# Seven block products beside each FFN1 step, and block sums a few steps earlier

## The chip, the cores and the metric

One core of one Trainium2 chip. The metric is the device time of one launch in microseconds. TensorE (PE) does matrix products into PSUM; VectorE (DVE), ScalarE (ACT) and GpSimd (POOL) do the rest, and SyncE (SP) issues output transfers. Each engine works through its own list of instructions in order, and semaphores keep the lists in step.

## The reference

Attention over 8 batches, 8 heads, 576 queries of 64 elements, with 16 beacon keys that all queries see and 576 causal ones. Its output is laid out as 4608 tokens of 512, and a feed-forward layer follows:

```python
x = attn_out.transpose(0, 2, 1, 3).reshape(B * S, H * D)      # 4608 x 512
h = x @ w_in                                                  # 4608 x 2048
g = np.where(h > 0.0, h, np.exp(np.minimum(h, 0.0)) - 1.0)
return g @ w_out                                              # 4608 x 512
```

## The kernel before, in words

Tokens are cut into ten tiles: two of 256, then eight of 512 (t = 2 to 9). The order of every engine's work is written out by hand. Short words name the operations, with their arguments behind dots, and a function `run` emits them one by one; what is emitted first stands first on its engine. For tiles 0 to 2 the words are one long string. From there on a loop goes over blocks b = 3 to 10. Block b does FFN1 of tile b, FFN2 of tile b − 1, and parts of the attention of batches b and b + 1; blocks 8 and 9 have no attention left, and block 10 has only FFN2 of tile 9.

A block has 16 steps, i = 0 to 15, one for each 128 columns of h:

- `F` (line 436): four matmuls of 128 x 512 into one of two PSUM banks, `hps`.
- `e` (446, ScalarE): the exponential of the bank. `r` (451, VectorE): min(e, 1) − 1. `g` (459, VectorE): the larger of h and r, into the tile `gt`. Then the bank is free for the F two steps later.
- `S`, `x`, `m` (277, 287, 303): scores, their exponential on ScalarE, the causal mask on VectorE. `T`, `ck` (235, 256): transposes of q and k and their copy on ScalarE. `L`, `W`, `R` (314): row sums and products with v, R being those of the last 64 queries of a batch. `n` (347, 350): reciprocal of the row sums as exp(−ln) on ScalarE. `M` (384, 404, VectorE): the scaled output, which is x of FFN1. Twelve steps carry such work: eight with scores (0, 1, 4, 5, 7, 8, 11, 12) and four with transposes and products (2, 6, 9, 13).

FFN2 of a tile is a product of 2 x 2 blocks (tokens halved, 2048 halved by alternating chunks, 512 halved) in Winograd's form, with seven block products where eight would be plain. Each product is a phase `ph` = 0 to 6 of 16 matmuls: two halves `qd` of 128 tokens, eight chunks `c` each. Phases 0, 2, 4, 6 write one PSUM bank and phases 1, 3, 5 another, some of them adding to what is there. `Q` (531) emits the matmuls, and `J` what follows a phase: a copy to `sm` on ScalarE (540; phases 0, 2, 3), a sum with it on VectorE (547; phases 1, 4, 5) or a copy on ScalarE (545; phase 6), the last two kinds with a store of 256 KB on SP's queue.

The left operands are blocks of g and sums of them. `Z` (489, VectorE) makes four sums, each in two halves of four chunks: sum 3 into `s3`, sums 1, 2 and 4 in place. Sum 2 overwrites the operand of phase 0 and is the operand of phase 2; sum 4 does the same between phases 1 and 5; sum 1 is for phase 3, sum 3 for phase 4. `wt` (also 489) makes the sums of the weights, once.

Before the change `Q` has a phase and a half as arguments and emits eight matmuls. A list `HS` gives the 14 steps that have one; steps 6 and 13 have none. `J` follows the second half of its phase in the same step, and `Z` stands behind `J`, in the steps that `SUMS` gives. Phases 0 to 6 so end in steps 1, 3, 5, 8, 10, 12 and 15. Words in a step are emitted as F, e, r, g, then Q and J, then Z, then the attention work.

Of the kernel before, what the change touches and what calls it, by code (L numbers as in the profile page):

```python
# [17 lines left out]
def kernel(  # L18
# [21 lines left out]
    R = 6  # L40
# [29 lines left out]
    NFC = DF // P  # L70
# [31 lines left out]
    NPR = NFC // 2  # L102
# [381 lines left out]
    def A(t, h_, j, i):  # L484
        v_ = gh[t, h_].rearrange("p (c j) (i w) -> p c j i w", j=2, i=2)
        return v_[:, :, j, i, :]
# [19 lines left out]
    def Z(t, n, h_):  # L506
# [8 lines left out]
        else:  # L515
# [3 lines left out]
    PH = [(0, (0, 0), B11, True), (1, (1, 0), B21, True), (0, (0, 0), T2, False), (1, (0, 1), T1, True),  # L519
          (0, None, B12, False), (1, (1, 0), B22, False), (0, (1, 1), T4, False)]  # L520

    @step
    def Q(t, ph, qd):

        if (t, 0) not in xy:
            for n_ in (0, 1) if t % 2 == 0 else (1, 0):
                xy[t, n_] = psum.tile([P, 2, HM], FP32, tag="ops", name="ops")
        n_, src, wt_, first = PH[ph]
        for c in range(NPR):
            lw = s3[:, c] if src is None else A(t, c // HP, *src)[:, c % HP]  # L530
            nc.tensor.matmul(  # L531
                out=xy[t, n_][:, qd, :], lhsT=lw[:, P * qd:P * (qd + 1)], rhs=wt_[:, c, :],
                start=(first and qd == 0 and c == 0), stop=(c == NPR - 1), skip_group_check=True)
# [33 lines left out]
    def run(names):  # L567
        for word in names.split():
            f, *args = word.split(".")
            op[f](*[a if a in "ABR" else int(a) for a in args])  # L570
# [30 lines left out]
    M.2.0.1 e.2.7 M.2.0.0 F.2.9 wt.1.1 S.3.0.0 e.2.9 S.2.3.2 lv.3 G.1.0.2 r.2.7 g.2.7 x.3.0.0 x.2.3.2  # L601
    F.2.11 wt.2.0 S.3.0.1 e.2.11 x.3.0.1 r.2.9 m.3.0.0 g.2.9 m.2.3.2 r.2.11 g.2.11 s.1.1 S.2.3.3 m.3.0.1
    F.2.10 wt.2.1 x.2.3.3 G.1.0.3 e.2.10 S.3.0.2 m.2.3.3 o.1.0 x.3.0.2 S.3.0.3 F.2.12 wt.4.0 r.2.10 m.3.0.2 g.2.10
    L.2.1 e.2.12 W.2.1.0 x.3.0.3 s.1.0 r.2.12 F.2.14 wt.4.1 g.2.12 m.3.0.3 n.2.1 M.2.1.0 F.2.13 e.2.14
    T.3.1 W.2.1.1 e.2.13 r.2.14 R.2 ck.3.1 T.3.2 g.2.14 r.2.13 F.2.15 g.2.13 M.2.1.1 n.2.R M.2.R
    e.2.15 r.2.15 ck.3.2 g.2.15
    """)

    def T_(b, p):
        if b < B:  # L610
            run(f"cb.{b}.{p} T.{b}.{p} ck.{b}.{p}")

    def SC(b, p, g0):
        if b < B:
            for g_ in (g0, g0 + 1):
                run(f"S.{b}.{p}.{g_} x.{b}.{p}.{g_} m.{b}.{p}.{g_}")

    def LW(b, g):
        run(f"L.{b}.{g} W.{b}.{g}.0 n.{b}.{g} M.{b}.{g}.0")

    def WR(b, g):
        run(f"W.{b}.{g}.1" + g * f" R.{b}" + f" M.{b}.{g}.1" + g * f" n.{b}.R M.{b}.R")

    SLOTS = [0, 1, 2, 4, 5, 6, 7, 8, 9, 11, 12, 13]
    HS = [0, 1, 2, 3, 4, 5, 7, 8, 9, 10, 11, 12, 14, 15]
    SUMS = {0: [(-1, 1, 1)], 2: [(-1, 2, 0)], 3: [(-1, 2, 1)], 5: [(-1, 4, 0)], 7: [(-1, 4, 1)],
            11: [(0, 3, 0)], 13: [(0, 1, 0)], 15: [(0, 3, 1)]}
    for b in range(3, NT // TT + 2):
        todo = {}
        if b < B:  # L630
            todo = dict(zip(SLOTS, [
                lambda: SC(b, 1, 0), lambda: SC(b, 1, 2), lambda: (T_(b, 3), LW(b, 0)),
                lambda: SC(b, 2, 0), lambda: SC(b, 2, 2), lambda: (T_(b + 1, 0), WR(b, 0)),
                lambda: SC(b, 3, 0), lambda: SC(b, 3, 2), lambda: (T_(b + 1, 1), LW(b, 1)),
                lambda: SC(b + 1, 0, 0), lambda: SC(b + 1, 0, 2), lambda: (T_(b + 1, 2), WR(b, 1))]))
        if b == 3:
            run("wt.3.0 wt.3.1 Z.2.3.0 Z.2.1.0 Z.2.3.1")
        for i in range(NFC):
            if b < len(tiles):
                run(f"F.{b}.{i} e.{b}.{i} r.{b}.{i} g.{b}.{i}")  # L640
            if i in HS:
                n_ = HS.index(i)
                run(f"Q.{b - 1}.{n_ // 2}.{n_ % 2}")
                if n_ % 2:
                    run(f"J.{b - 1}.{n_ // 2}")
            for dt_, n_, h_ in SUMS.get(i, []):
                if b + dt_ < len(tiles):
                    run(f"Z.{b + dt_}.{n_}.{h_}")
            if i in todo:
                todo[i]()  # L650
            if i == 3 and b + 1 < B:
                run(f"lk.{b + 1} lv.{b + 1}")
# [28 lines left out]
```

## Time and profile before

| what | value |
|---|---|
| time, median of 3 | 377.95 us (377.32 to 377.96) |
| profiled execution | 377.59 us, its span 375.9 us |
| PE busy | 352.2 us |
| DVE busy | 286.5 us |
| ACT busy | 253.7 us |
| block with attention (b=5, first F to first F) | 184.01 to 224.37 us |
| block without attention (b=9) | 330.38 to 358.09 us |

In rows of the profile, L531 is line 531 of the kernel, `ops<-wt,gt` reads tiles wt and gt and writes ops, and a bracket gives the idle time before and what ended it. Rows in order of time begin with the start and the duration, both in us. Matmuls are pipelined: the duration of a row reaches beyond the start of the next, so the distance of starts is what one costs. Rows of stretches give the stretch, its length, and busy time of each engine with its number of instructions in brackets. Waits give the sum in us, how many, and the longest.

### The profile page before, as it was taken

Reading aid. Unit: us, or ns where it says so; the run is one execution under the profiler, and the core shown is the slowest. Engines: PE = TensorE matmul, PEld = TensorE weight load, DVE = VectorE, ACT = ScalarE, POOL = GpSimd, SP = SyncE. Lnnn points to the kernel's source line nnn. Section 1 sums busy time; section 2 is a strip of 40 time slices with the busy share of each in tenths; the row PEclk is TensorE's granted clock in tenths of the full one; section 3 lists DMA queues with packets and bytes.
Section 4 is the critical chain, followed back from the end, with each engine's and each line's share of the span. In section 5 each row is a group of like instructions: output and inputs, shape, how many; then the busy total and the mean of one; then the engine's idle time right before and its main releaser. Section 6 shows DMA issues by size and latency. Waiting matters only on the chain.

```text
span 375.9 us, 11164 instructions
## 1 busy us (share of the span) xinstructions
PE 352.2 (94%) x4811; PEld 219.8 (58%) x4811; DVE 286.5 (76%) x675; ACT 253.7 (67%) x383; POOL 68.5 (18%) x100
## 2 busy tenths in 40 slices
PE   7989999999888999899989999899989998998985
PEld 3567666454555665566655666566645665665674
DVE  2448877779788697787877787868878888888861
ACT  2999996887676867697668768686767354344321
POOL 8876630410330004100510040000000000000000
PEclk9999999999999999999999999999999999999998
DMA  8999999963298019900973057001000100110112
GB/s 117 170 186 197 179 190 196 74 103 81 17 59 149 3 58 95 151 6 30 102 101 77 14 71 70 28 2 59 31 28 2 60 28 30 47 39 29 56 58 85
DMA packets 65201, 28.89 MB, mean 77 GB/s; under 512 B 41088, under 2 KB 63616, under 8 KB 65152
## 3 DMA queue, kind: packets, MB, share of 16 engines
q0 software_dynamic: 54720, 18.49, 44.7%
q1 hardware_dynamic: 9856, 9.57, 7.7%
q8 instruction: 37, 0.61, 0.7%
q10 hardware_dynamic: 576, 0.13, 0.2%
q14 instruction: 12, 0.10, 0.1%
HBM read 37.22 MB, written 9.44 MB: 124 GB/s over the span
## 4 chain that ended last, share of the span: by engine, by line
PE 57%; DVE 20%; ACT 10%; issue 5%; POOL 3%; DMA 3%; ACTq 0%; DVEq 0%; POOLq 0%
PE hps L436 22%; PE ops L531 18%; DVE gt L459 5%; PE lt L314 5%; PE sc L277 5%; ACT et L287 4%; DVE r L451 4%; PE ops L468 3%; DVE xT L384 3%; PE tp L235 3%; DVE osb L547 3%; DVE gt L489 2%; DMA kst<-in_k_dram 2%; PE ut L314 2%; ACT rl L350 2%
## 5 line engine op out<-in xcount | busy, mean ns | idle before, releaser
L436 PE MATMUL hps<-xT,w_in 128*128 128x512 f16 (+1 forms) x640 | 147.7, 359 | 4.4 <-DVE gt L459 3.5
L446 ACT ACTIVATE e<-hps 128x512 f32<-128x512 f32 x144 | 86.5, 601 | 53.4 <-PE hps L436 52.2
L287 ACT ACTIVATE et<-sc 128x832 f16<-128x832 f32 x128 | 104.2, 873 | 21.3 <-PE sc L277 21.3
L459 DVE TENSOR_TENSOR gt<-hps,r 128x512 f16<-128x512 f32 x144 | 99.6, 691 | 6.5 <-PE sc L277 0.5
L531 PEld LDWEIGHTS <-gt 128*128 128x128 f16 x768 | 74.5, 98 | 38.0 <-DVE gt L489 11.5
L436 PEld LDWEIGHTS <-w_in 128*128 128x128 f16 x640 | 56.3, 97 | 51.7 <-issue 12.0
L451 DVE TENSOR_SCALAR r<-e 128x512 f16<-128x512 f32 x144 | 62.5, 434 | 16.2 <-ACT e L446 14.4
L531 PE MATMUL ops<-wt,gt 128*128 128x256 f16 x384 | 50.5, 273 | 9.3 <-DVE gt L489 9.3
L303 DVE TENSOR_TENSOR et<-et,triu 128x256 f16<-128x256 f16 (+2 forms) x164 | 39.8, 271 | 23.3 <-ACT et L287 21.8
L531 PE MATMUL ops<-w_out,gt 128*128 128x256 f16 x384 | 49.1, 273 | 0.0
L277 PE MATMUL sc<-qk 64*128 64x208 bf16 (+9 forms) x528 | 36.6, 249 | 2.0 <-ACT et L287 1.1
L256 ACT COPY qk<-tp 128x1152 bf16<-128x1152 bf16 x29 | 32.5, 1134 | 3.9 <-PE tp L235 3.8
L132 POOL DMA_DIRECT2D v<-in_v_dram x40 | 34.2, 885 | 4.6 <-DMA kst<-in_k_dram 2.6
L489 DVE TENSOR_TENSOR gt<-gt 128x1024 f16<-128x1024 f16 x48 | 32.5, 682 | 0.1
L277 PEld LDWEIGHTS <-qk 64*128 64x128 bf16 x528 | 19.0, 94 | 22.6 <-issue 16.0
L314 PEld LDWEIGHTS <-v 128*32 128x32 f16 x1248 | 21.2, 94 | 9.2 <-issue 2.5
L127 POOL DMA_DIRECT2D v<-in_beacon_v_dram x8 | 4.3, 534 | 115.0 <-PE ut L314 115.0
L384 DVE TENSOR_TENSOR xT<-lt,rl 128x448 f16<-128x448 f32 (+6 forms) x28 | 10.6, 419 | 15.4 <-ACT rl L350 15.4
L547 DVE TENSOR_TENSOR osb<-ops,sm 128x512 f32<-128x512 f32 x24 | 16.4, 682 | 5.6 <-issue 4.6
L540 ACT COPY sm<-ops 128x512 f32<-128x512 f32 x24 | 14.1, 586 | 8.3 <-PE ops L531 8.3
L314 PE MATMUL ut<-et,v 128*32 128x64 f16 (+6 forms) x840 | 16.9, 224 | 1.1 <-issue 0.6
L468 PE MATMUL ops<-w_out,gt 128*128 128x512 f16 x64 | 16.5, 380 | 0.0
(55 smaller groups left out, 249.2 us busy)
## 6 DMA issues: line engine op xcount, KB each, us to landing
out_dram<-osb SPq DMA_DIRECT2D x36, 256.0 KB, 2.2
qst<-in_q_dram POOLq DMA_DIRECT2D x6, 576.0 KB, 6.5
kst<-in_k_dram POOLq DMA_DIRECT2D x6, 576.0 KB, 9.4
v<-in_v_dram POOLq DMA_DIRECT2D x24, 128.0 KB, 5.1
w_in<-in_moe_w_in_dram POOLq DMA_DIRECT2D x16, 128.0 KB, 5.3
w_out<-in_moe_w_out_dram POOLq DMA_DIRECT2D x4, 512.0 KB, 11.0
v<-in_v_dram POOLq DMA_DIRECT2D x8, 112.0 KB, 3.3
v<-in_v_dram POOLq DMA_DIRECT2D x8, 80.0 KB, 5.2
```

What stands on the lines that cost most here:

```text
L132: nc.gpsimd.dma_start(out=st[b][2][r0:r0 + n, j, :, :], in_=v[b, :, ilo[j]:ilo[j] + n, :].rearrange("h s d -> s h d"),)
L256: nc.scalar.copy(out=t[:, :, NB:SK].rearrange("c i (p r) -> c i p r", r=R), in_=tps[b, p][:, :, 0:S].rearrange("c i (r p) -> c i p r", r=R))
L277: nc.tensor.matmul(out=s[:, h, a - c0:e - c0], lhsT=t[D * h:D * (h + 1), 1, P * j:P * (j + 1)], rhs=t[D * h:D * (h + 1), 0, NB + qa + a - ...
L287: nc.scalar.activation(out=ets[b, p][:, :, GW * g:GW * (g + 1)], in_=sc[b, p, g][:, :, 0:GW], func=AFT.Exp, bias=0.0, scale=SCALE)
L303: nc.vector.tensor_tensor(out=o, in0=o, in1=triu[0:kc[j], :, t0:t0 + e - a], op=ALU.mult)
L314: nc.tensor.matmul(out=t[32 * i:32 * (i + 1), a - qa:e - qa], lhsT=ones[0:kc[j], :] if half is None else v16[0:kc[j], j, h, 32 * half:32 * ...
L436: nc.tensor.matmul(out=h[:, n_, :], lhsT=w_in16[:, cc, P * fc:P * (fc + 1)], rhs=xt[k][:, cc, a - TT * k:e - TT * k], start=(cc == 0), sto ...
L446: nc.scalar.activation(out=eb[t, i], in_=flat(hp[t, i]), func=AFT.Exp, bias=0.0, scale=1.0)
L451: nc.vector.tensor_scalar(out=rb[t, i], in0=eb[t, i], scalar1=1.0, scalar2=1.0, op0=ALU.min, op1=ALU.subtract)
L459: nc.vector.tensor_tensor(out=gh[k][:, i % UN, :], in0=flat(hp[t, i]), in1=rb[t, i], op=ALU.max)
L489: nc.vector.tensor_tensor(out=o_, in0=a_, in1=b_, op=op_)
L531: nc.tensor.matmul(out=xy[t, n_][:, qd, :], lhsT=lw[:, P * qd:P * (qd + 1)], rhs=wt_[:, c, :], start=(first and qd == 0 and c == 0), stop= ...
```

## The change

`Q` has a first and a last matmul, counted through all seven phases (112), and each of the 16 steps emits seven. `J` is emitted in the step in which the last matmul of its phase was emitted, behind that step's matmuls: phases 0 to 6 in steps 2, 4, 6, 9, 11, 13 and 15. The second half of sum 4 moves from step 7 to 6, and the first half of sum 1 from 13 to 12. For tile 2 the three sums that stood at the start of block 3 move into the written order: `Z.2.3.0` behind g of step 12, `Z.2.1.0` behind g of step 14, and `Z.2.3.1` behind the last g. The matmuls, their operands and their order stay the same.

```diff
-    def Q(t, ph, qd):
+    def Q(t, k0, k1):
...
-        n_, src, wt_, first = PH[ph]
-        for c in range(NPR):
+        for k_ in range(k0, k1):
+            ph, qd, c = k_ // (2 * NPR), k_ // NPR % 2, k_ % NPR
+            n_, src, wt_, first = PH[ph]
...
-    L.2.1 e.2.12 W.2.1.0 x.3.0.3 s.1.0 r.2.12 F.2.14 wt.4.1 g.2.12 m.3.0.3 n.2.1 M.2.1.0 F.2.13 e.2.14
-    T.3.1 W.2.1.1 e.2.13 r.2.14 R.2 ck.3.1 T.3.2 g.2.14 r.2.13 F.2.15 g.2.13 M.2.1.1 n.2.R M.2.R
-    e.2.15 r.2.15 ck.3.2 g.2.15
+    L.2.1 e.2.12 W.2.1.0 x.3.0.3 s.1.0 r.2.12 F.2.14 wt.4.1 g.2.12 Z.2.3.0 m.3.0.3 n.2.1 M.2.1.0 F.2.13 e.2.14
+    T.3.1 W.2.1.1 e.2.13 r.2.14 R.2 ck.3.1 T.3.2 g.2.14 Z.2.1.0 r.2.13 F.2.15 g.2.13 M.2.1.1 n.2.R M.2.R
+    e.2.15 r.2.15 ck.3.2 g.2.15 Z.2.3.1
...
-    HS = [0, 1, 2, 3, 4, 5, 7, 8, 9, 10, 11, 12, 14, 15]
-    SUMS = {0: [(-1, 1, 1)], 2: [(-1, 2, 0)], 3: [(-1, 2, 1)], 5: [(-1, 4, 0)], 7: [(-1, 4, 1)],
-            11: [(0, 3, 0)], 13: [(0, 1, 0)], 15: [(0, 3, 1)]}
+    NQ = 14 * NPR // NFC
+    SUMS = {0: [(-1, 1, 1)], 2: [(-1, 2, 0)], 3: [(-1, 2, 1)], 5: [(-1, 4, 0)], 6: [(-1, 4, 1)],
+            11: [(0, 3, 0)], 12: [(0, 1, 0)], 15: [(0, 3, 1)]}
...
-            run("wt.3.0 wt.3.1 Z.2.3.0 Z.2.1.0 Z.2.3.1")
+            run("wt.3.0 wt.3.1")
...
-            if i in HS:
-                n_ = HS.index(i)
-                run(f"Q.{b - 1}.{n_ // 2}.{n_ % 2}")
-                if n_ % 2:
-                    run(f"J.{b - 1}.{n_ // 2}")
+            run(f"Q.{b - 1}.{NQ * i}.{NQ * (i + 1)}")
+            for ph in range(7):
+                if NQ * i < 2 * NPR * (ph + 1) <= NQ * (i + 1):
+                    run(f"J.{b - 1}.{ph}")
```

## The prediction

> **What bounds the kernel now.** I read the busy shares first, then the waits of TensorE, then stretches of one block each, then rows in order of time.
>
> ```profile
> PE 352.2 (94%) x4811; PEld 219.8 (58%) x4811; DVE 286.5 (76%) x675; ACT 253.7 (67%) x383; POOL 68.5 (18%) x100
> ```
> ```profile
> PE ops L531 <- DVE gt L489: 9.3, 8, 1.3
> PE hps L436 <- DVE gt L459: 3.5, 6, 1.7
> ```
> ```profile
> 143.63:184.01 40.38, 39.02 (x576) 24.48 (x576) 32.18 (x78) 30.04 (x46) 6.28 (x9) 1.00 0.53 72
> 302.68:330.38 27.70, 26.53 (x176) 17.09 (x176) 24.02 (x44) 11.53 (x20) 0.00 (x0) 1.00 0.11 38
> ```
>
> TensorE is busy for 94% of the span, and nearly all it waits for in the second half is VectorE: eight waits of the block products (Q, line 531) for block sums (Z, line 489), and six of FFN1 (F, line 436) for g (line 459), whose PSUM banks it takes over. The two stretches are one block with attention (b=4: 40.38 us, PE 39.02, DVE 32.18, ACT 30.04) and one without (b=8: 27.70 us, PE 26.53, DVE 24.02). Busy matmuls overlap, so I take lost time from starts. On TensorE, without attention (b=8, steps 3 to 7) and at its first step:
>
> ```profile
> 302.68 1.02 PE L436 MATMUL hps<-xT,w_in 128*128 128x512 f16 x4 [0.41 <-DVE gt L459]
> ...
> 307.88 1.03 PE L436 MATMUL hps<-xT,w_in 128*128 128x512 f16 x4
> 308.75 1.04 PE L531 MATMUL ops<-w_out,gt 128*128 128x256 f16 x8
> 309.62 1.03 PE L436 MATMUL hps<-xT,w_in 128*128 128x512 f16 x4
> 310.49 0.60 PE L531 MATMUL ops<-wt,gt 128*128 128x256 f16 x4
> 311.99 0.61 PE L531 MATMUL ops<-wt,gt 128*128 128x256 f16 x4 [0.90 <-DVE gt L489]
> ...
> 314.17 2.19 PE L436 MATMUL hps<-xT,w_in 128*128 128x512 f16 x8
> ```
>
> Four F matmuls take 0.87 us and eight Q matmuls 0.87, one behind the other with nothing between: 0.109 us for one Q matmul, and a change from F to Q or back costs nothing. Then the third phase breaks off after four matmuls. With attention (b=5), on TensorE and on VectorE:
>
> ```profile
> 186.30 1.04 PE L436 MATMUL hps<-xT,w_in 128*128 128x512 f16 x4
> ...
> 188.61 1.04 PE L436 MATMUL hps<-xT,w_in 128*128 128x512 f16 x4
> ...
> 194.11 1.03 PE L436 MATMUL hps<-xT,w_in 128*128 128x512 f16 x4
> 194.97 0.60 PE L531 MATMUL ops<-wt,gt 128*128 128x256 f16 x4
> 196.87 0.61 PE L531 MATMUL ops<-wt,gt 128*128 128x256 f16 x4 [1.29 <-DVE gt L489]
> ```
> ```profile
> 194.92 0.69 DVE L459 TENSOR_TENSOR gt<-hps,r 128x512 f16<-128x512 f32 x1
> 195.53 0.68 DVE L547 TENSOR_TENSOR osb<-ops,sm 128x512 f32<-128x512 f32 x1
> 196.13 0.68 DVE L489 TENSOR_TENSOR gt<-gt 128x1024 f16<-128x1024 f16 x1
> ```
>
> Phase 2 begins at step 4, and its fifth matmul reads the second half of sum 2. That sum is issued at step 3, but behind J of phase 1 (line 547), which is issued in the same step and takes 0.60 us of VectorE; all of that stands behind g. So the sum ends at 196.13 + 0.68 = 196.81, and the matmul starts 0.06 later.
>
> **The change part by part.** *Removed: the wait in phase 2.* Four matmuls should take 0.43 us. With attention they take 196.87 − 194.97 = 1.90, a loss of 1.46; without it 1.50, a loss of 1.07. In the last block, which has no F:
>
> ```profile
> 361.58 0.60 PE L531 MATMUL ops<-wt,gt 128*128 128x256 f16 x4
> 363.19 3.23 PE L531 MATMUL ops<-wt,gt 128*128 128x256 f16 x28 [1.00 <-DVE gt L489]
> ```
>
> 1.61 − 0.43 = 1.17. Five blocks have attention (b=3 to 7), two have none: 5 × 1.46 + 2 × 1.07 + 1.17 = 10.6 us. The idle in the rows agrees: 5 × 1.29 + 2 × 0.90 + 1.00 = 9.25 beside the 9.3 of the waits.
>
> With seven matmuls a step, phase 1 ends in step 4, so J of phase 1 is issued there, behind the sum. Phase 2's fifth matmul becomes the second of step 5. How late the sum then is follows from the way of one step from F to g:
>
> ```profile
> 308.95 0.60 ACT L446 ACTIVATE e<-hps 128x512 f32<-128x512 f32 x1 [1.14 <-PE hps L436]
> ...
> 309.58 0.43 DVE L451 TENSOR_SCALAR r<-e 128x512 f16<-128x512 f32 x1
> ...
> 310.04 0.69 DVE L459 TENSOR_TENSOR gt<-hps,r 128x512 f16<-128x512 f32 x1
> ```
>
> F starts at 307.88; e 1.07 later, r 1.70, g 2.16 (ends 2.85), the next VectorE instruction 2.77. The sum of step 3 thus ends 2.77 + 0.68 = 3.45 after F of step 3. A bare step is now 0.87 + 7 × 0.109 = 1.63; the matmul comes at 2 × 1.63 + 0.87 + 0.11 = 4.24. Spare 0.8, more with attention. In the last block the sum is the third behind another one and g, so it ends 2.77 + 3 × 0.6 + 0.68 = 5.25 after F of step 15, and the matmul comes at 1.63 + 36 × 0.109 = 5.55: spare 0.3. I take all eight waits as gone.
>
> *Moved: products into steps 6 and 13.* They had none, so F of 7 followed F of 6 at once: two F in 2.19 where 2 × 0.87 + 0.16 = 1.90 is due, a loss of 0.29 while g of step 5 frees the bank. Twice in each block without attention: 1.2 us. Now F comes 3.26 after the F two steps before and needs g's end at 2.85: cover 0.41. One VectorE instruction of 0.60 a step just fits (2.77 + 0.60 = 3.37 beside the next r at 1.63 + 1.70 = 3.33). Step 11 now has two (J of phase 4, sum 3): the next r is 0.64 late, and F of step 14 waits 0.64 − 0.41 = 0.23 in each such block. Saved 1.2 − 0.5 = 0.7.
>
> With attention these steps get 0.76 more of TensorE ahead of transposes and attention products, and the others 0.11 less; the total of matmuls is the same. Before, a block's end ran like this (VectorE; then TensorE: F of step 13, and of step 0 of b=5):
>
> ```profile
> 182.30 0.49 DVE L404 TENSOR_TENSOR xT<-ut,rl 128x128 f16<-128x128 f32 x2 [0.74 <-ACT rl L350]
> ...
> 183.27 0.69 DVE L459 TENSOR_TENSOR gt<-hps,r 128x512 f16<-128x512 f32 x1
> ```
> ```profile
> 176.99 1.04 PE L436 MATMUL hps<-xT,w_in 128*128 128x512 f16 x4
> ...
> 184.01 1.02 PE L436 MATMUL hps<-xT,w_in 128*128 128x512 f16 x4
> ```
>
> The rest R of attention, its ln and exp, the product M (line 404), then r and g of step 14 stand in one line, and g ends at 183.96, just ahead of the next block's F. From F of 13 to that F it is 7.02, of which 0.18 is waiting (starts of 13 to 15 give 6.84). After: 6.84 + 0.76 − 2 × 0.11 = 7.38. The line in front: R is 0.76 later but VectorE had been 0.45 behind it, so g ends 6.97 + 0.3 to 0.4 = 7.3. The borders now lose 0.55, 0.18, 0.23, 0.23 and 0.58 (302.68 is the last), 1.8 together. I keep 0.2 in the first and 0.5 in the last, where no transposes lengthen step 13: saved 1.1.
>
> *Moved: three sums of block 3 into the hand-written order.* Now five stand in a row ahead of its first r (VectorE, then TensorE; the first row is the idle stretch ahead of them):
>
> ```profile
> 99.86 0.76 DVE L384 TENSOR_TENSOR xT<-ut,rl 128x384 f16<-128x384 f32 x2 [1.10 <-PE ut L314]
> ...
> 103.23 1.28 DVE L489 TENSOR_TENSOR w_out<-w_out 128x1024 f16<-128x1024 f16 x2
> 104.43 0.69 DVE L489 TENSOR_TENSOR s<-gt 128x1024 f16<-128x1024 f16 x1
> ...
> 106.36 0.42 DVE L451 TENSOR_SCALAR r<-e 128x512 f16<-128x512 f32 x1
> ```
> ```profile
> 105.37 0.53 PE L277 MATMUL sc<-qk 64*128 64x208 bf16 x10
> 107.56 1.02 PE L436 MATMUL hps<-xT,w_in 128*128 128x512 f16 x4 [1.66 <-DVE gt L459]
> ```
>
> The third one stays in the row (it only changes place with the two of `wt`), so r comes 2 × 0.6 earlier, and F with it: 107.56 becomes 106.35. A step with scores takes 2.31 (186.30 to 188.61), of which F and Q are 1.74; 0.57 goes to the scores, 0.1 of it ahead of them. So F could have started at 105.37 + 0.46 = 105.83, and two matmuls earlier now, 105.61. The wait falls from 1.73 to 0.74: saved 1.0. The two that leave take 1.2 us in front of an idle stretch of 1.10: that covers them; uncovered they would cost 1.2.
>
> *Other moves.* J of phases 0, 2, 3 (ScalarE) go from steps 1, 5, 8 to 2, 6, 9; J of 4 and 5 and their stores on SP's queue one step later. SP carries nothing else, and the loads of step 3 pass nothing. The nearest reader is phase 6, which writes the bank that J of 4 reads, at 3.26 + 0.87 + 0.55 = 4.68 after F of 11; J ends at 3.45. On ScalarE (b=5):
>
> ```profile
> 187.74 0.60 ACT L446 ACTIVATE e<-hps 128x512 f32<-128x512 f32 x1
> 188.25 0.59 ACT L540 COPY sm<-ops 128x512 f32<-128x512 f32 x1
> 188.73 1.62 ACT L287 ACTIVATE et<-sc 128x832 f16<-128x832 f32 x2
> 190.23 0.62 ACT L446 ACTIVATE e<-hps 128x512 f32<-128x512 f32 x1
> ```
>
> A step with scores takes ScalarE 2.49 with a J and 2.01 without; TensorE took 2.31 and takes 2.20 now. Every J leaves those steps, so ScalarE keeps pace, by 0.19.
>
> **Sum.** 10.6 + 0.7 + 1.1 + 1.0 = 13.4 us. The profiled execution took 377.59 (span 375.9), 0.36 under the median of 377.95 and inside its runs: 377.6 − 13.4 = 364.2.
>
> The Trainium skill ("Perfetto Trace Analysis", Identifying the Most-Contended Engine) holds matmul busy time to be a poor measure and asks for the share of weight loads: by that, 58% here, TensorE is far from full, and a hole on it need not set the end. By that rule the sum could stay at 377.6; by the starts above it is 364.2, since outside the holes F and Q abut to 0.01 us.
>
> **The rivals.** *Scores take over* (steps with scores become ScalarE's): the spare is only 0.19, and the next scores wait for a buffer that the exponential frees. For it: the loop 2.01; against: nothing waits there now although two such steps a block take 2.49. If the loop were 2.30, 0.1 is lost in each of 38 such steps (8 in each of four blocks, 6 in the fifth): 364.2 + 3.8 = 368.0. *The sum stays late*: in front of g of step 3 stands an M that waits for ScalarE; if that is 1.5 late, half the wait stays, 5 × 0.7 = 3.5: 367.7. Against it: the spare is 0.8. *TensorE is not the limit*: what the holes give is taken elsewhere, 377.6. Against it: DVE has 32.18 and ACT 30.04 of busy time in a block that would take 40.38 − 1.46 − 0.2 = 38.7. *Slower*: the line at the block's end. R 0.76 later, J of 5 (0.6) not paid for by sum 1 moved up, 0.64 carried over from step 11, and the transposes' copy in front of ln (1.1) make g 3.1 later, less 0.41 of cover: 2.7 in each of five blocks, 13.5, and the 1.1 of the borders is not saved: 364.2 + 14.6 = 378.8. It decides from 2.9 us of delay; I count 0.4.
>
> **How the numbers follow.** Forecast 0.76 (362 to 366.5), scores 0.10, late sum 0.05, not the limit 0.05, slower 0.04. If every hole named were gone, 15.2 us, it would be 362.4, and other small waits of about 1 us could go with them: low end 361.6. The high end takes in both 368 cases: 368.8. About 0.2% is what a measurement can tell from no change: faster 0.91, same 0.05, slower 0.04.
>
> **What would show it.** No wait of line 531 for line 489 over 0.2 us; blocks with attention at 38.7, without at 26.3; the last sum 2 ahead of J on VectorE; F of step 2 in block 3 near 106.3. It is wrong if new waits of scores for line 287, or of F for line 459 at block ends, exceed 0.5 us a block.

## The result, and the profile after

The changed kernel takes 363.98 us (median of four runs, 363.15 to 364.36) beside 377.69 for the kernel before on the same chip: a ratio of 0.963, with a 95% interval of 0.961 to 0.966. The profiled execution took 364.15 us, its span 362.4. The forecast was 364.2.

The busy shares and the waits of TensorE, after (J, Q and their copies stand one line further down: Q is line 532):

```profile
PE 350.6 (97%) x4811; PEld 219.9 (61%) x4811; DVE 284.5 (78%) x675; ACT 254.6 (70%) x383; POOL 68.2 (19%) x100
```
```profile
PE hps L436 <- DVE gt L459: 2.4, 7, 0.5
```

There is no row any more in which Q waits for a sum (line 489). Three blocks as stretches, b=4, b=6 and b=8:

```profile
140.81:179.68 38.87, 38.63 (x577) 24.32 (x576) 32.49 (x78) 30.92 (x47) 6.98 (x10) 1.00 0.59 78
...
218.54:257.08 38.54, 38.53 (x576) 24.34 (x576) 31.71 (x77) 30.52 (x46) 1.49 (x2) 1.00 0.29 42
...
293.28:319.65 26.37, 26.25 (x176) 17.20 (x176) 23.51 (x43) 11.57 (x20) 0.00 (x0) 1.00 0.10 33
```

In block 6 TensorE is busy for all but 0.01 of 38.54 us. From first F to first F the blocks took:

| block | 3 | 4 | 5 | 6 | 7 | 8 | 9 | 10 to the end |
|---|---|---|---|---|---|---|---|---|
| before, us | 42.39 | 40.38 | 40.36 | 40.36 | 37.94 | 27.70 | 27.71 | 17.8 |
| after, us | 39.14 | 38.87 | 38.86 | 38.54 | 36.20 | 26.37 | 26.35 | 16.4 |

The blocks gained 13.9; block 3 began 0.44 later (101.67, before 101.23), which leaves the 13.5 by which the spans differ. The place of the old wait in block 5, on VectorE and on TensorE:

```profile
190.26 0.69 DVE L459 TENSOR_TENSOR gt<-hps,r 128x512 f16<-128x512 f32 x1
190.87 0.68 DVE L489 TENSOR_TENSOR gt<-gt 128x1024 f16<-128x1024 f16 x1
...
192.53 0.68 DVE L548 TENSOR_TENSOR osb<-ops,sm 128x512 f32<-128x512 f32 x1
```
```profile
190.20 0.60 PE L532 MATMUL ops<-w_out,gt 128*128 128x256 f16 x4
190.64 0.49 PE L532 MATMUL ops<-wt,gt 128*128 128x256 f16 x3
...
192.40 0.93 PE L532 MATMUL ops<-wt,gt 128*128 128x256 f16 x7
```

The sum stands right behind g of step 3 and ends at 191.55. Its reader, the second matmul of the group at 192.40, is due at 192.51: 0.96 to spare. J of phase 1 comes at 192.53, a step later.

### The profile page after: what moved, and what is told of

Same layout as the page of the kernel before. It is cut to its first block, busy times and chain, and to the rows that moved or that the text cites. A ratio compares the mean times of both kernels' runs of the same rounds, so it can differ in the third digit from the quotient of the medians.

```text
span 362.4 us, 11165 instructions
## 1 busy us (share of the span) xinstructions
PE 350.6 (97%) x4811; PEld 219.9 (61%) x4811; DVE 284.5 (78%) x675; ACT 254.6 (70%) x383; POOL 68.2 (19%) x100
## 4 chain that ended last, share of the span: by engine, by line
PE 72%; DVE 11%; DMA 6%; POOL 4%; issue 2%; ACT 2%; ACTq 0%; POOLq 0%
PE hps L436 29%; PE ops L532 23%; PE sc L277 6%; DMA kst<-in_k_dram 5%; PE lt L314 4%; PE tp L235 4%; PE ut L314 3%; DVE gt L459 3%; DVE r L451 3%; PE ops L468 2%; DMA qst<-in_q_dram 2%; DVE xT L384 1%; POOL w_in L144 1%; POOL v L132 1%; DVE s L489 1%
## 5 line engine op out<-in xcount | busy, mean ns | idle before, releaser
L287 ACT ACTIVATE et<-sc 128x832 f16<-128x832 f32 x128 | 104.1, 871 | 13.5 <-PE sc L277 12.0
L451 DVE TENSOR_SCALAR r<-e 128x512 f16<-128x512 f32 x144 | 63.9, 444 | 13.8 <-ACT e L446 11.9
L532 PE MATMUL ops<-wt,gt 128*128 128x256 f16 x384 | 52.5, 273 | 0.0
L532 PE MATMUL ops<-w_out,gt 128*128 128x256 f16 x384 | 51.4, 273 | 0.0
L303 DVE TENSOR_TENSOR et<-et,triu 128x256 f16<-128x256 f16 (+2 forms) x164 | 38.7, 269 | 15.9 <-ACT et L287 15.3
L384 DVE TENSOR_TENSOR xT<-lt,rl 128x448 f16<-128x448 f32 (+6 forms) x28 | 10.6, 419 | 15.9 <-ACT rl L350 15.9
L548 DVE TENSOR_TENSOR osb<-ops,sm 128x512 f32<-128x512 f32 x24 | 16.4, 682 | 4.4 <-issue 3.3
L532 PE MATMUL ops<-w_out,s 128*128 128x256 f16 x128 | 17.6, 273 | 0.0
```

Of the source, the lines that this page charges most:

```text
L287: nc.scalar.activation(out=ets[b, p][:, :, GW * g:GW * (g + 1)], in_=sc[b, p, g][:, :, 0:GW], func=AFT.Exp, bias=0.0, scale=SCALE)
L303: nc.vector.tensor_tensor(out=o, in0=o, in1=triu[0:kc[j], :, t0:t0 + e - a], op=ALU.mult)
L451: nc.vector.tensor_scalar(out=rb[t, i], in0=eb[t, i], scalar1=1.0, scalar2=1.0, op0=ALU.min, op1=ALU.subtract)
L532: nc.tensor.matmul(out=xy[t, n_][:, qd, :], lhsT=lw[:, P * qd:P * (qd + 1)], rhs=wt_[:, c, :], start=(first and qd == 0 and c == 0), stop= ...
```

## The experiments

### The sum ahead of J, nothing else

```diff
             if i in HS:
                 n_ = HS.index(i)
                 run(f"Q.{b - 1}.{n_ // 2}.{n_ % 2}")
+                if i == 3:
+                    run(f"Z.{b - 1}.2.1")
                 if n_ % 2:
...
-                if b + dt_ < len(tiles):
+                if b + dt_ < len(tiles) and i != 3:
```

> The kernel before, with eight products in 14 steps as it was; only in step 3 the second half of sum 2 is emitted ahead of J of phase 1. My theory (the wait is one J of 0.60 us on VectorE plus too few matmuls between the sum and its reader): the sum ends 0.60 earlier, so the wait shrinks from 1.46 to 0.86 with attention, from 1.07 to 0.47 without, and is gone in the last block: 5 x 0.6 + 2 x 0.6 + 1.17 = 5.4 less, 372.3 us. Rival, only the order counts: all eight waits gone, 10.6 less, 367.1. Rival, only the even spread counts: 377.7.

Measured: 371.92 us (371.33 to 372.84), ratio 0.984 (0.982 to 0.987). The waits, and the place in block 5 on TensorE:

```profile
PE ops L531 <- DVE gt L489: 4.1, 7, 0.7
```
```profile
193.52 0.60 PE L531 MATMUL ops<-wt,gt 128*128 128x256 f16 x4
194.82 0.39 PE L531 MATMUL ops<-wt,gt 128*128 128x256 f16 x2 [0.69 <-DVE gt L489]
```

Seven waits are left, and the last block's is gone. Here 1.30 − 0.43 = 0.87 is lost where 0.86 was expected. The order on VectorE alone gives 5.7 us (377.63 for the kernel before on this chip).

### Seven a step, with the sum behind J

```diff
-    SUMS = {0: [(-1, 1, 1)], 2: [(-1, 2, 0)], 3: [(-1, 2, 1)], 5: [(-1, 4, 0)], 6: [(-1, 4, 1)],
+    SUMS = {0: [(-1, 1, 1)], 2: [(-1, 2, 0)], 4: [(-1, 2, 1)], 5: [(-1, 4, 0)], 6: [(-1, 4, 1)],
```

> The changed kernel, seven products a step, with the second half of sum 2 in step 4 instead of 3, so again behind J of phase 1. My theory: the sum then ends 4.05 + 0.68 after F of step 4 less the start of that chain; with attention it ends near 193.8 where its reader is due at 192.5, a wait of 1.35; without attention 303.9 against 302.4, 1.55; the last block 1.2. Together 5 x 1.35 + 2 x 1.55 + 1.2 = 11.0 more than 364.0: 375.0 us. Rival, the spread alone made the gain and the sum's place is of no weight: 364 to 366.

Measured: 372.4 us (371.98, 372.38 and 373.88; a fourth run of 1511.69, four times as long, is left out, and nothing on record explains it), ratio 0.986 (0.983 to 0.989). The waits, and block 5 on VectorE and on TensorE:

```profile
PE ops L532 <- DVE gt L489: 7.5, 8, 1.3
```
```profile
193.36 0.68 DVE L548 TENSOR_TENSOR osb<-ops,sm 128x512 f32<-128x512 f32 x1
193.96 0.68 DVE L489 TENSOR_TENSOR gt<-gt 128x1024 f16<-128x1024 f16 x1
```
```profile
193.66 0.27 PE L532 MATMUL ops<-wt,gt 128*128 128x256 f16 x1
194.70 0.83 PE L532 MATMUL ops<-wt,gt 128*128 128x256 f16 x6 [0.77 <-DVE gt L489]
```

All eight waits are back, behind J as before. With attention the reader comes 1.04 − 0.11 = 0.93 late and not 1.35 as I wrote: I had left out that the sum, once gone from step 3, lets r and g of step 4 start earlier. In whole times the sum ahead of J with eight a step gains 5.7 us, seven a step with the sum behind J 5.3, and both together 13.7. But the 5.3 hold the change's other gains too, those of block 3, of the borders and of steps 6 and 13. At the place of the wait alone, by distances of starts over all eight phases, 10.6 us are lost before, 5.2 with the order alone, 8.8 with seven a step alone and nothing with both. Seven a step alone so gains 1.7 there and the order alone 5.3. Together they gain more than the sum of the two, since only both put the reader behind the end of the sum.

### The other two moved sums

```diff
-    ... 6: [(-1, 4, 1)],
-            11: [(0, 3, 0)], 12: [(0, 1, 0)], 15: [(0, 3, 1)]}
+    ... 7: [(-1, 4, 1)],
+            11: [(0, 3, 0)], 13: [(0, 1, 0)], 15: [(0, 3, 1)]}
```

> The changed kernel with the second half of sum 4 back in step 7 and the first half of sum 1 back in step 13. My theory: step 13 then has J of phase 5 and a sum on VectorE ahead of M, r and g of step 14, so g of step 14 is 0.6 later; the border of a block with attention waits 0.4 to 0.6 more (four of them, and the fifth), and in the blocks without attention F of the next block's first step waits 0.2 more: 2.5 to 3 more, 366.8 us. Rival, these two moves do nothing by themselves: 364.0.

Measured: 363.89 us (363.08 to 364.15). My theory fell: the rival's 364.0 is what came. Block 4 of this kernel as a stretch:

```profile
139.81:178.68 38.87, 38.63 (x577) 24.33 (x577) 31.89 (x78) 30.85 (x47) 7.24 (x10) 1.00 0.58 77
```

It takes 38.87 as in the changed kernel; from first F to first F blocks 3 to 8 take 39.34, 38.87, 38.87, 38.74, 35.98 and 26.37, 0.2 us more at two places and 0.2 less at one. Most of the 0.6 of VectorE in step 13 finds cover that I had not counted: at the border of blocks 4 and 5 the last M (line 404) starts 5.90 us after F of step 13, beside 5.70 in the changed kernel. Behind blocks 3 and 6 the 0.2 that is left does cost 0.2. Behind blocks 4 and 5 it does not show, because there r of step 14, which stands beside loads that GpSimd issues, takes 0.55 us instead of 0.76:

```profile
177.35 0.55 DVE L451 TENSOR_SCALAR r<-e 128x512 f16<-128x512 f32 x1
```

That is luck and no cover. In the time these two moves are worth nothing that can be measured here.

### Block 3's sums back at its start

```diff
-    ... r.2.12 F.2.14 wt.4.1 g.2.12 Z.2.3.0 m.3.0.3 ...  g.2.14 Z.2.1.0 r.2.13 ...  g.2.15 Z.2.3.1
+    ... r.2.12 F.2.14 wt.4.1 g.2.12 m.3.0.3 ...  g.2.14 r.2.13 ...  g.2.15
...
-            run("wt.3.0 wt.3.1")
+            run("wt.3.0 wt.3.1 Z.2.3.0 Z.2.1.0 Z.2.3.1")
```

> The changed kernel with the three sums of tile 2 back at the start of block 3. My theory: r of step 0 stands behind five sums again, F of step 2 in block 3 waits 1.2 longer (gap of 1.8 instead of 0.64 ahead of it): 365.1 us. Rival, the wait is covered by what follows or the prologue pays it back: 364.0.

Measured: 366.04 us (365.09 to 367.66), 2.1 more than the changed kernel where 1.1 was expected. The profiled execution is the longest one, 367.66. TensorE in block 3, and a stretch of it with the granted clock (the column behind the five engines):

```profile
108.58 1.65 PE L436 MATMUL hps<-xT,w_in 128*128 128x512 f16 x4 [1.87 <-DVE gt L459]
110.02 1.70 PE L532 MATMUL ops<-w_out,gt 128*128 128x256 f16 x7
```
```profile
110.00:112.00 2.00, 2.00 (x18) 1.25 (x18) 1.97 (x6) 1.07 (x2) 0.00 (x0) 0.50 0.00 0
```

The wait is as expected, 1.87 beside the 0.51 of the changed kernel. But behind it the clock fell to 0.50, from 108.8 to 112.2, and seven Q matmuls and a switch took 1.63 where they take 0.85. That is 3.4 us at half speed, 1.7 us lost, in this execution: without it 367.66 would be 366.0, near the other runs. The run of 366.04 has as low a mean clock (0.994); the three with 0.998 and more took 365.09 to 366.23, that is 1.1 to 2.2 more than the 364.0 of the changed kernel. The kernel before had a wait of 1.66 at this place and kept the clock at 1.00.

### GpSimd's loads away from a block's end

```diff
-    stage.tile([P, NKC, H, D], FP16, tag="v16", name="v16")
+    stage.tile([P, NKC, H, D], FP16, tag="v16", name="v16", bufs=3)
...
-            sm[t, ph] = melt.tile([P, 2, HM], FP32, tag="sm", name="sm")
+            sm[t, ph] = melt.tile([P, 2, HM], FP32, tag="sm", name="sm", bufs=2)
```

In the changed kernel, at the border of blocks 4 and 5, on VectorE, GpSimd and TensorE:

```profile
178.14 0.76 DVE L451 TENSOR_SCALAR r<-e 128x512 f16<-128x512 f32 x1
178.94 0.69 DVE L459 TENSOR_TENSOR gt<-hps,r 128x512 f16<-128x512 f32 x1
```
```profile
176.94 4.23 POOL L132 DMA_DIRECT2D v<-in_v_dram  x5
```
```profile
178.51 0.93 PE L532 MATMUL ops<-wt,gt 128*128 128x256 f16 x7
179.68 1.02 PE L436 MATMUL hps<-xT,w_in 128*128 128x512 f16 x4 [0.24 <-DVE gt L459]
```

r takes 0.76 us there while GpSimd issues loads of v, and the next F starts 1.17 after seven Q matmuls that take 0.76.

> The changed kernel with three buffers for v instead of two (and two instead of three for sm, to make room), so that GpSimd issues the loads of v in steps 3 to 5 and not behind R at a block's end. In the changed kernel r of step 14 takes 0.76 instead of 0.42 in two of the blocks with attention, while GpSimd issues a load of v, and the next block's F waits 0.45 there. My theory: the two coincide because GpSimd holds r up; r goes back to 0.42, both borders lose 0.1 or nothing: 363.3 us, and a long r may turn up in steps 3 to 5 where it has cover. Rival, chance: r of step 14 stays at 0.76 and the time at 364.0.

Measured: 364.12 us (362.60 to 367.82), no difference in time. In the trace the theory holds. r at the same border, then step 3 to 5 of block 4 on VectorE and GpSimd, then block 4:

```profile
182.42 0.43 DVE L451 TENSOR_SCALAR r<-e 128x512 f16<-128x512 f32 x1
```
```profile
155.21 0.75 DVE L451 TENSOR_SCALAR r<-e 128x512 f16<-128x512 f32 x1
...
156.60 0.68 DVE L489 TENSOR_TENSOR gt<-gt 128x1024 f16<-128x1024 f16 x1
157.20 0.51 DVE L451 TENSOR_SCALAR r<-e 128x512 f16<-128x512 f32 x1
```
```profile
153.99 4.20 POOL L132 DMA_DIRECT2D v<-in_v_dram  x5
```
```profile
145.08:183.62 38.54, 38.54 (x577) 24.32 (x576) 32.07 (x78) 30.73 (x46) 6.25 (x8) 1.00 0.56 76
```

The long r moved with the loads, to a place where nothing waits for it, and blocks 4 and 5 take 38.54 and 38.57 with no wait of TensorE in them. The 0.6 us so gained are less than the scatter of what comes before: block 3 began at 106.01 in this execution and at 101.67 in the changed kernel's. Most of that delay is a wait for a load of k and a stretch of half clock right behind it:

```profile
53.51 0.45 PE L235 MATMUL tp<-identb,kst 96*64 96x96 bf16 x12 [1.76 <-DMA kst<-in_k_dram]
```
```profile
54.30:57.60 3.30, 3.30 (x20) 1.99 (x18) 1.12 (x2) 1.41 (x2) 0.98 (x2) 0.50 1.93 172
```

The third buffer need not be the cause: the run without the mask, further down, has two buffers for v and the same wait (2.04 us, to 52.77) with half clock behind it.

### One sum from step 11 to step 10

```diff
-            11: [(0, 3, 0)], 12: [(0, 1, 0)], 15: [(0, 3, 1)]}
+            10: [(0, 3, 0)], 12: [(0, 1, 0)], 15: [(0, 3, 1)]}
```

> The changed kernel with the first half of sum 3 in step 10 instead of 11, so no step has J and a sum behind each other on VectorE between steps 7 and 15. My theory: the wait of F of step 14 in the two blocks without attention (0.33 each) goes, and part of the border of block 7 to 8 (0.35): 0.7 to 1.0 less, 363.1 us. Rival: the wait moves one step on, or comes from the chain of g alone: 364.0.

Measured: 363.27 us (362.88 to 364.32). Blocks 7 and 8:

```profile
255.91:292.51 36.60, 35.90 (x490) 22.29 (x488) 30.44 (x69) 24.42 (x39) 0.00 (x0) 1.00 0.10 31
292.51:318.54 26.03, 26.03 (x178) 17.22 (x176) 23.48 (x43) 11.64 (x20) 0.00 (x0) 1.00 0.11 36
```

Block 8 takes 26.03 instead of 26.37, with no wait left. Block 7 took 0.4 longer in this execution: a hole of 0.8 us opened inside the small matmuls of R, which waited for nothing that the profile names. So the waits went as expected; the time, 0.7 us less, lies inside the scatter of both kernels.

### Less work for TensorE, less work for VectorE

```diff
         for k_ in range(k0, k1):
+            if 24 <= k_ < 28:
+                continue
```

> The changed kernel without four of the seven matmuls of step 3 (phase 1, the first four of its second half: left out of the result), in all eight blocks; all other engines have the same work. TensorE as the limit: 8 x 4 x 0.109 = 3.5 less, 360.5 us. Rival, TensorE is not the limit (the share of weight loads is 61%): 363.5 to 364, the time reappears as waits of TensorE.

Measured: 362.13 us (361.58 to 364.76), 1.9 less and not 3.5. Blocks 4 and 6, and TensorE in R of block 6:

```profile
139.21:177.66 38.45, 38.22 (x574) 23.93 (x573) 32.31 (x78) 30.92 (x47) 6.97 (x10) 1.00 0.60 78
216.10:254.96 38.86, 38.28 (x573) 23.98 (x573) 31.53 (x77) 30.52 (x46) 1.48 (x2) 1.00 0.29 41
```
```profile
251.36 0.35 PE L314 MATMUL ut<-et,v 80*32 80x64 f16 x21 [0.58 <-issue]
```

Blocks 3, 4 and 5 are each 0.42 shorter, all that was taken out. Block 6 has one of the holes without a name in R: its step 13 takes 0.76 us longer, more than the 0.43 taken out. In block 7 (36.11, 0.1 less) scores wait 0.3 longer for the PSUM buffer of M, and block 8 gave 0.2 of 0.43, the rest going to F behind g: without attention the chain by e, r and g is close behind TensorE. So in blocks 3 to 5 TensorE is the limit; in block 8, without attention, it is so for 0.2 us only. The 1.9 us in the time are less sure than the block times, since block 3 began at 100.50 here and at 101.67 in the changed kernel's profile.

```diff
-        for (j, qa, qe, col) in lays[b]:
+        for (j, qa, qe, col) in lays[b] if b < 4 else []:
```

> The changed kernel without the causal mask for batches 4 to 7 (left out of the result): some 80 VectorE instructions of 0.2 to 0.29 us, 19 us of VectorE in blocks 3 to 7. TensorE as the limit: only the few waits of F for g in those blocks can go, 0.5 to 1.5 less, 362.5 to 363.5 us. Rival, VectorE is the limit or shares it: 10 to 19 less, 345 to 354.

Measured: 364.20 us (363.69 to 367.28), nothing gained. Block 4:

```profile
143.74:182.60 38.86, 38.63 (x577) 24.33 (x576) 28.73 (x58) 30.91 (x47) 6.97 (x10) 1.00 0.59 78
```

VectorE has 28.73 us of work instead of 32.49, and the block takes 38.86 instead of 38.87. The work of VectorE counts only where an instruction stands in front of one that TensorE waits for.

### All of it, twice

With three buffers for v, sum 3 in step 10, and the two weight sums of block 3's start moved to its steps 7 and 8, emitted behind the attention work:

```diff
-        if b == 3:
-            run("wt.3.0 wt.3.1")
...
+            if b == 3 and i in (7, 8):
+                run(f"wt.3.{i - 7}")
```

> The changed kernel with three buffers for v (two for sm), the first half of sum 3 in step 10, and the two weight sums that stand at the start of block 3 moved to its steps 7 and 8 (their reader is phase 4, from step 9). My theory: the waits of the borders behind blocks 4 and 5 (0.34 each by the runs before), of step 14 in the two blocks without attention (0.33 each) and of step 2 in block 3 (0.5 of its 0.64) go: 1.8 less than the changed kernel, 362.2 us beside 364.0. Rival: these waits are taken up by the next ones in line, or the new places of the sums open others: 363.5 to 364.

> The changed kernel once more, unchanged, on the same chip as the one with three edits: 363.5 to 364.4 us, the scale for a difference of one or two microseconds. No theory says anything else.

Measured: 364.02 us (363.05 to 364.58) beside 364.02 (363.60 to 364.96) for the changed kernel again. Among the waits is a new one:

```profile
PE ops L532 <- DVE w_out L489: 1.1, 1, 1.1
```

Phase 4 now waits for the second weight sum, which stood on VectorE behind the masks of steps 7 and 8, one of which had waited 0.48 us for ScalarE. Block 3 takes 39.80 where it takes 39.14 in the changed kernel: the moved work made the very kind of wait that the change had removed, and the rival's time is what came. With steps 1 and 7 instead, ahead of the attention work:

```diff
+            if b == 3 and i in (1, 7):
+                run(f"wt.3.{i // 7}")
             if i in todo:
```

> The three edits again, with the two weight sums in steps 1 and 7 of block 3 and ahead of the attention work of those steps (before they stood in steps 7 and 8 behind it, and phase 4 waited 1.30 us for the second). My theory: that wait goes, block 3 takes 38.5 instead of 39.8, and with 38.54 for blocks 4 to 6 and 26.04 for the two without attention the kernel takes 362.1 us. Rival: the prologue's scatter of a microsecond hides it, 363 to 364, with the block times as said.

Measured: 363.45 us (361.40 to 363.92). A stretch early on, block 3 and block 8:

```profile
25.90:29.30 3.40, 3.40 (x23) 2.18 (x23) 0.17 (x2) 1.72 (x3) 3.24 (x5) 0.51 1.01 160
102.80:141.35 38.55, 38.55 (x577) 24.36 (x576) 33.24 (x82) 31.71 (x49) 6.24 (x8) 1.00 0.53 69
293.25:319.29 26.04, 26.04 (x178) 17.22 (x176) 23.48 (x43) 11.65 (x20) 0.00 (x0) 1.00 0.11 36
```

The blocks are as expected, and TensorE is busy all through them. But this execution had 3.4 us of half clock near 26 us and began block 3 at 102.80, 1.7 later than the changed kernel's second profile (101.09). From there to the end it takes 259.2 us beside 260.8. The 1.7 are what 3.4 us at half speed cost. The medians, from two chips, differ by 0.6, inside the scatter of both: better in the traces by 1.6 us, not shown in the time, as the rival had it.

## Why the prediction was right, point by point

- *The wait in phase 2, 10.6 us.* Right, in size and in cause. All eight are gone; bringing back J ahead of the sum brings all eight back, and the order alone removes just what the 0.60 of J accounts for.
- *The spare of 0.8 between sum and reader.* 0.96 in block 5, where I had said more with attention.
- *Steps 6 and 13 without attention, 0.7 us.* The step is right, the size a little high: F of step 14 waits 0.28 (316.34, behind two matmuls from 315.84) instead of 0.23, and the block takes 26.37 beside 26.3. The cause named, two VectorE instructions in step 11, is shown by the run that parts them: 26.03.
- *The borders, 1.1 us.* Here the working failed: the five borders lost 1.75 us before and lose 1.24 now, so 0.5 is saved. I took r at 0.42 us everywhere; at the borders of blocks 4 and 5, and 5 and 6, it takes 0.76 beside GpSimd's loads, and 0.4 us remain at each where I had written none. With r as I had taken it the border is free (38.54 in the run with three buffers), so the chain itself was counted rightly.
- *Block 3's sums, 1.0 us.* F of step 2 started at 106.66, which is 106.22 after the later start is taken off, beside 106.35. Two matmuls (0.22) that stood ahead of it come later now, so of the 1.34 by which F is earlier 1.1 is saved. Taking the move back costs 1.36 of waiting, and can cost more by the clock.
- *Not counted.* Step 6 with attention gave 0.2 a block. Before, the transposes followed F at once (block 5, step 6, before and then after):

```profile
200.18 1.04 PE L436 MATMUL hps<-xT,w_in 128*128 128x512 f16 x4
201.22 0.45 PE L235 MATMUL tp<-identb,qst 96*64 96x96 bf16 x12
...
202.67 0.61 PE L436 MATMUL hps<-xT,w_in 128*128 128x512 f16 x2
```
```profile
193.72 1.04 PE L436 MATMUL hps<-xT,w_in 128*128 128x512 f16 x4
...
195.46 0.45 PE L235 MATMUL tp<-identb,qst 96*64 96x96 bf16 x12
...
196.78 0.39 PE L436 MATMUL hps<-xT,w_in 128*128 128x512 f16 x1
```

  The step took 2.49 and takes 3.06 with 0.76 more of matmuls: 0.19 of small holes around the transposes is covered now. That the waits behind it were for a PSUM buffer was not tested.
- *The sum.* By distances of starts the terms came to 10.6 (the wait), 0.6 (steps 6 and 13 without attention), 0.5 (borders), 1.1 (block 3) and 1.0 (step 6 with attention, five blocks). The last, which the sum did not have, and the 0.6 missing at the borders nearly cancel; that 13.5 measured stands beside 13.4 is in part luck, and nearer than the terms were.
- *The rivals.* Scores did not become ScalarE's: its waits on TensorE for line 287 fell from 21.3 to 12.0 us in all but did not go, from block 3 on no row shows scores of TensorE waiting for line 287, and no block with attention is over 38.87 but block 3. The late sum did not come. That TensorE is not the limit, as the share of weight loads (61% after) would have it, is not borne out: taking 3.8 us of VectorE out of a block changes nothing, and taking 0.43 of TensorE out shortens blocks 3 to 5 by 0.42 each. The slower case would have needed g of step 14 to come 2.9 us later at each border. At the border of blocks 4 and 5 it ends 7.67 after F of step 13 (178.94 + 0.69 − 171.96), beside 6.97 before: 0.7 later where I had counted 0.4, and F waits 0.4 for it.

## What to carry to other kernels

On a full engine look at what the instruction that it waits for has in front of it in its own queue: here a result's copy of 0.60 us, of no hurry, stood ahead of an operand's sum. Such a wait goes when the urgent instruction comes first and the reader comes late enough; of the 10.6 us of this wait the order alone took away 5.3 and the later reader alone 1.7. Work moved off one place must be followed to the next reader of each thing it makes, as the weight sum in step 8 showed: block 3 took 39.80 us with it and 38.55 with the two weight sums in steps 1 and 7.

## What the hardware showed that was not expected

- r (VectorE, 512 elements from f32 to f16, all in SBUF) takes 0.42 us and up to 0.91 while GpSimd issues loads: in the changed kernel's profile all nine that took over 0.5 us lie on such an issue, though not every one beside an issue is longer. The sums, with two f16 operands, keep 0.68 in the same stretches. The Trainium skill ("SBUF — State Buffer", SBUF: two separate sides) states that VectorE in a two-port mode and GpSimd lock each other out of a shared pair of ports for whole instructions; the run with three buffers agrees, since the long r moved with the loads. That r runs in such a mode no run here shows.
- TensorE's clock went to 0.50 for 3.4 us, with work at hand, in four of the thirteen profiled executions. Three times it did so within 0.8 us of the end of an idle stretch: of 1.87 us (block 3's sums back), of 1.76 (three buffers for v) and of 2.04 (no mask). The fourth, at 25.9 us of the last kernel, had no idle stretch above 0.67 us ahead of it, and stretches of 1.66 us in the kernel before and 1.65 in the run with the sum ahead of J did not do it. So the length of one stretch does not decide alone. The Trainium skill ("TensorE: Matmul & The Clock Gate", HAM oscillation) warns of idle stretches above about 3.4 us; here shorter ones were enough.
- Trains of 80 small matmuls (R) have a hole of 0.2 to 1.0 us now and then that no semaphore explains. Every profiled execution has one in the train just ahead of block 3, at 98.6 to 104.2 us; others come and go, such as those at 289 us in block 7 (sum 3 in step 10: 288.97) and at 251 us (TensorE with less work). In the traces' records of transfers, one of 16 KB on the queue for instructions starts 1.0 to 1.9 us behind each of these holes, mostly 1.1. That points at the supply of instructions, but no run tested it, and the cause stays open.
